# A weight's float built in place in SBUF, its low part formed by GpSimd, the skip score's product in a bank of its own, and a new table for the planner

## The chip, the cores and the metric

The kernel runs on one core of one Trainium2 chip. The core has five engines that run side by side, each through its own queue in order: TensorE (PE in the profile) multiplies matrices, VectorE (DVE), ScalarE (ACT) and GpSimd (POOL) work element by element, and SyncE (SP) issues the transfers between HBM and SBUF. Products land in PSUM, which has eight banks of 512 floats for each of 128 partitions. The metric is the device time of one execution in microseconds; less is better.

## The reference

Three layers follow each other. Shapes: batch 4, 8 heads, 768 positions, head size 48, so 3072 tokens of width 384; the middle layer is 2048 wide.

```python
# 1: a recurrence with a complex decay for each head and channel
mag = np.sqrt(a_re * a_re + a_im * a_im)
scale = np.minimum(mag, 0.999) / (mag + 1e-06)
...
    S_re, S_im = (new_re + kv, new_im)
    y[:, :, t] = np.einsum('bhd,bhde->bhe', q[:, :, t], S_re)
# 2: a wide layer with a rational function
h = x @ w_in
P = a[0] + a[1] * h + a[2] * h2 + a[3] * h3
Q = 1.0 + np.abs(b[0]) * np.abs(h) + np.abs(b[1]) * h2
g = P / (Q + 1e-06)
return (g @ w_out).astype(np.float32)
# 3: experts, for those tokens alone whose skip score is above 0
skip_score = x @ w_skip
do_compute = skip_score > 0
```

## The kernel before

The tokens are cut into 24 chunks of 128; two chunks are a unit, so there are 12 units. For each unit the first layer runs in chunk form. An "early" chain (e1 to e13, ScalarE and VectorE in turn, lines 442 to 453) forms logarithms and angles of the decay; an arc tangent (L484) and two sines (L478, L479) follow, each with a reload of ScalarE's function table; TensorE forms prefix sums (L545 to L575); key and query products kt and qt (L327), transposes (L619) with their evictions (L625), scores (L637), masks, products with v and the state (L663, L665) and the update of the state (L684) give y. GpSimd, VectorE or ScalarE then split y into a high and a low part (xh, xl; L716 to L721).

The second layer runs in steps: 8 for a unit, 96 in all, each for 256 tokens and 256 of the 2048 middle channels. G1 (L766) is two groups of nine products (three inputs times high-high, low-high, high-low), G2 (L812) two groups of six that are accumulated in two PSUM banks `ob` over a unit's 8 steps. Between them stand, for each step, ScalarE's a1 to a5 (L752, L324), VectorE's d1 to d4 (L756) and the split into gh (L795) and gl (L798). The step buffers are threefold: G1 of step s+3 waits for d4 of step s. The first step's G1 needs xh and xl of both chunks of unit 0. The other six PSUM banks, `zb`, are handed out by the planner.

The weights are float64 in memory. The function `weight` turns each piece of 128 x 384 into a float32 and splits it into a high and a low part (wih, wil, woh, wol). A double's two 32-bit words lie side by side: `lw` and `hw` are views with a stride of two words over the staging buffer. wb1 (L353) and wb2 (L356) gather low bits and sign in a `zb` bank, wy (L360) scales the upper word, wb3 (L363) joins both into that bank, whi (L371) rounds it to the high part, wlo (L373) subtracts. There are 16 pieces of w_in (steps 0 to 7, two each) and 16 of w_out, so 32 in all, and all of them belong to the first unit.

The order on every engine is decided when the kernel is built: `Plan.order` plays the tasks through with a cost for each choice of engine, a due time and the numbers of the table `PP` (slacks, biases, engines ruled out for a task in `NO`, due times of steps), and the instructions are emitted in the order it finds. So a changed cost or table changes the order on all engines.

At a unit's end, ScalarE or VectorE evicts the two `ob` banks to `x2b` (named ev), which is stored; sk (L330) multiplies `ob` by w_skip in place and sums it into `skip`. After the last unit `flags` adds up what the later paths would have to do; in the trace no instruction of them runs.

Of the kernel before, what the change touches and what calls it, by code (L numbers as in the profile page):

```python
# [10 lines left out]
F32 = mybir.dt.float32  # L11
# [146 lines left out]
PP = dict(P0=5.749, P1=7.419, NO={'kr': ('ACT', 'POOL'), 'wy': ('ACT', 'DVE'), 'e4': ('ACT',), 'ev': ('POOL',), 'xabs': ('DVE',), 'cadd8': ('DVE',), 'xpe': ('POOL',), 'xlo': ('ACT',), 'msk': ('POOL',), 'whi': ('POOL',), 'qr': ('ACT', 'DVE'), 'prr2': ('DVE',), 'prr1': ('ACT', 'DVE'), 'gh': ('ACT', 'DVE'), 'cadd': ('ACT', 'DVE'), 'gl': ('DVE',), 'yev': ('DVE',)}, E0=-7.632, E1=-9.777, TC=40, WS=(0, 1, 2, 3, 4, 5, 0, 1, 1, 0, 1, 2, 2, 1, 2, 2), HO={('d2b', 'ACT'): 0.618, ('msk', 'ACT'): 0, 'DVE': 0.349, 'POOL': 0}, DW=88.344, WL=9, P=5.802, LAG2=4.955, SL={'ACT': 0.3, 'DVE': 3.115, 'POOL': 1.396, 'SP': 1.011, 'PE': 1.871, '2': 2.358}, X1=13.588, T0=107.458, NZ=6, NH=3, CU=2, BI={'DVE': 7.051, 'POOL': 17.078})  # L158


def main_part(tc, ctx, q, k, v, a_re, a_im, w_in, w_out, moe_a, moe_b, w_skip, out, keep):
# [176 lines left out]
    def weight(keys, tag, stg, hi, lo, key, part, shape=lambda x: x):  # L338

        n = DM  # L340
        h_, w_ = (tag + ("h",), ("wz", tag[0], part % 2))
        tk = ("wz",) + key
        if wide:
            rw = stg.bitcast(I32).rearrange("p (n z) -> p n z", z=2)
            lw, hw = rw[:, :, 0], rw[:, :, 1]
            hf = hw.bitcast(F32)

            def bits():
                return zb[pl.slot[tk]][:, 0:n].bitcast(I32)
# [13 lines left out]
            pl.add([("DVE", 0.48, lambda: nc.vector.scalar_tensor_tensor(  # L363
                out=bits(), in0=hw, scalar=3, in1=bits(), op0=ALU.logical_shift_left, op1=ALU.bitwise_or))],
                reads=keys + [h_], writes=[w_], name="wb3")
            src, fr = [w_], tk
        else:
            def t():
                return shape(stg)
            src, fr = keys, None  # L370
# [58 lines left out]
    def early(u, cc):  # L429
        load_a(u, cc)  # L430
        w = len(cc) / 2
        fa, fd, fp = 0.73 if w == 1 else 0.43, 0.87 if w == 1 else 0.47, 1.76 if w == 1 else 0.94
# [56 lines left out]
    def cums(u, c):  # L489
# [7 lines left out]
        if not first and not summed:  # L497
            cr = cs[0:1, hs, 1, :]
            pl.add(dma((cr, xr[127:128, ps, :])), reads=[f"x{1 - c}"], writes=[f"cs{c}"], name=f"cry{ci}", xfer=0.03)
            def a0():  # L500
                return hd("ai", F32, u)[0:1, hs, :]

            def cadd():
                nc.gpsimd.tensor_scalar(out=cr, in0=cr, scalar1=-2.0 * math.pi, scalar2=1.0, op0=ALU.mult, op1=ALU.mult)
                nc.gpsimd.tensor_tensor(out=a0(), in0=a0(), in1=cr, op=ALU.add)
            pl.add([("POOL", 1.3, cadd), ("DVE", 0.5, lambda: nc.vector.scalar_tensor_tensor(
                out=a0(), in0=cr, scalar=-2.0 * math.pi, in1=a0(), op0=ALU.mult, op1=ALU.add), True)],
                   reads=[f"cs{c}"], writes=[f"ai{c}"], name="cadd")
# [5 lines left out]
        if split and c == 0:  # L514
# [12 lines left out]
            pl.add([("POOL", 0.92, lambda: thi("POOL")), ("ACT", 0.73, lambda: thi("ACT")),  # L527
# [63 lines left out]
        if ci % CPB != CPB - 1:  # L591
            pl.add([("POOL", 0.5, lambda: nc.gpsimd.tensor_copy(last[96:128], r1[96:128, c].rearrange("p h d -> p d h")))],
                   reads=[f"r1{c}"], writes=["last"], name="last")
            pl.add(dma(*[(dec[ci % ND][48 * z:48 * z + 48, :], last[127:128]) for z in range(2)]), reads=["last"], writes=[("dec", ci % ND)], name=f"dec{ci}")

    def qrkr(u):
        for c in range(2):
            hs = slice(8 * c, 8 * c + 8)
            pl.add([tt("POOL", 0.96, r1[:, c], r1[:, c], raw["q"][:, hs, :], ALU.mult),
                    tt("DVE", 0.47, r1[:, c], r1[:, c], raw["q"][:, hs, :], ALU.mult)],  # L600
                   reads=["q"], writes=[f"r1{c}"], name="qr")

    def prods(u, c):
        ci = 2 * u + c
        csl = cs[:, 8 * c:8 * c + 8]
        for nm, r, t, key in (("r2", r2, kt[ci % 2], ("kt", ci % 2)), ("r1", r1, qt[0], "qt")):
            i0 = r[:, c].unsqueeze(2).to_broadcast([128, 8, 2, 48])
            pl.add([tt("DVE", 0.87, t, i0, csl, ALU.mult), tt("POOL", 1.76, t, i0, csl, ALU.mult)],
                   reads=[f"{nm}{c}", f"cs{c}"], writes=[key], name="pr" + nm)
# [21 lines left out]
    def scores(ci, hf):  # L631
# [14 lines left out]
        pl.add([("POOL", 0.6, lambda: nc.gpsimd.affine_select(  # L646
# [49 lines left out]
    def yevac(ci):  # L696
# [45 lines left out]
    def step(s):  # L742
# [76 lines left out]
        if p == NP - 1:  # L819
            for t in range(2):  # L820
# [8 lines left out]
                pl.add([stt(0.55, o, o, fine["sg"], wsk, ALU.mult, ALU.mult, both=False, accum_out=skip[:, ti:ti + 1])],  # L829
                       reads=["wsk", "cf"], writes=[("o", t)], name="sk", due=at(1, 3))  # L830
# [435 lines left out]
```

## Time and profile before

| | us |
|---|---|
| median of 3 runs (669.85 to 672.43) | 672.06 |
| the profiled execution: its own time | 673.5 |
| its span, first to last instruction | 671.8 |
| TensorE busy | 615.5 (92%) |
| ScalarE busy | 570.0 (85%) |
| VectorE busy | 498.8 (74%) |
| GpSimd busy | 470.7 (70%) |

A row's duration contains overlap with its neighbours on the same engine, so a group of rows can be shorter than its sum. A bracket at a row's end gives the idle time of the engine before it and what ended that. "PEclk" or the granted clock is the share of TensorE's full clock; the mean over the span is 0.962.

### The profile page before, as it was taken

The page shows a single profiled execution, that of the slowest core. Times are in us where ns is not written, and L with a number is a line of the kernel's source. Part 1 is how long each engine was busy: PE and PEld are TensorE (multiplying, and loading weights), DVE is VectorE, ACT ScalarE, POOL GpSimd, SP SyncE. Part 2 cuts the span into 40 slices and gives each one's busy share as a digit, 9 for nine tenths or more (in the row PEclk, how much of TensorE's full clock was granted, in tenths as well). Part 3 has the DMA queues.
Part 4 walks back from the last instruction along what each step waited for, and adds up shares of the span by engine and source line. Part 5 has one row for each costly group of instructions (what it writes and reads, how often), then busy time and mean ns, then how long its engine had stood idle before and what let it go on. Part 6 is the DMA issues. An engine that isn't in the chain of part 4 may idle for free.

```text
span 671.8 us, 13043 instructions
## 1 busy us (share of the span) xinstructions
PE 615.5 (92%) x4772; PEld 586.5 (87%) x4772; DVE 498.8 (74%) x822; ACT 570.0 (85%) x962; POOL 470.7 (70%) x469
## 2 busy tenths in 40 slices
PE   0485599999999999999999999999999999999993
PEld 0273489999999999999999999999989999999993
DVE  6989979977768877776689687686598676565771
ACT  5858988997999998997999998997999996976770
POOL 5566567787887696875887797775977776754452
PEclk9758879999999999999999999999999999999998
DMA  9834232410311212111212112111213010000000
GB/s 304 294 108 135 72 105 64 145 36 18 97 36 47 67 39 76 48 27 53 70 39 84 28 40 68 44 40 52 60 40 98 13 40 4 1 27 4 13 13 30
DMA packets 52140, 43.32 MB, mean 64 GB/s; under 512 B 31201, under 2 KB 48993, under 8 KB 52065
## 3 DMA queue, kind: packets, MB, share of 16 engines
q1 hardware_dynamic: 52064, 42.38, 20.9%
q8 instruction: 39, 0.64, 0.4%
q14 instruction: 37, 0.30, 0.1%
HBM read 36.38 MB, written 4.72 MB: 61 GB/s over the span
## 4 chain that ended last, share of the span: by engine, by line
PE 79%; DVE 8%; ACT 7%; issue 2%; DMA 2%; POOL 1%; SPq 0%; POOLq 0%; ACTq 0%
PE zb L766 28%; PE ob L812 28%; PE zb L637 6%; PE zb L619 5%; PE zb L663 4%; PE zb L684 3%; PE zb L665 2%; DVE wk L756 1%; DMA xl<-in_moe_w_out_dram 1%; ACT wk L752 1%; DVE zb L353 1%; DVE ail L537 1%; PE zb L575 1%; DVE zb L363 1%; DVE ta L445 1%
## 5 line engine op out<-in xcount | busy, mean ns | idle before, releaser
L756 DVE SCALAR_TENSOR_TENSOR wk<-wk,cf,zb 128x512 f32<-128x512 f32 x192 | 142.4, 743 | 105.2 <-ACT zb L752 49.1
L766 PE MATMUL zb<-xh,wih 128*128 128x256 f32 x576 | 167.6, 291 | 8.2 <-DVE wk L756 8.2
L766 PE MATMUL zb<-xl,wih 128*128 128x256 f32 x576 | 163.4, 284 | 0.0
L766 PE MATMUL zb<-xh,wil 128*128 128x256 f32 x576 | 162.7, 282 | 0.0
L324 ACT ACTIVATE wk<-wk,cf 128x512 f32<-128x512 f32 x192 | 139.0, 724 | 1.5
L798 POOL TENSOR_TENSOR gl<-wk,gh 128x512 fp32r<-128x512 f32 x96 | 131.8, 1374 | 5.8
L812 PE MATMUL ob<-woh,gh 128*128 128x384 f32 x384 | 134.5, 350 | 0.0
L812 PE MATMUL ob<-woh,gl 128*128 128x384 f32 x384 | 130.3, 339 | 0.0
L812 PE MATMUL ob<-wol,gh 128*128 128x384 f32 x384 | 130.3, 339 | 0.0
L795 POOL TENSOR_SCALAR gh<-wk 128x512 fp32r<-128x512 f32 x96 | 64.0, 667 | 83.3 <-PE ob L812 67.0
L766 PEld LDWEIGHTS zb<-xh,wih 128*128 128x128 f32 x576 | 109.5, 190 | 11.8 <-DVE wk L756 8.4
L766 PEld LDWEIGHTS zb<-xl,wih 128*128 128x128 f32 x576 | 109.5, 190 | 0.3 <-POOL wk L360 0.3
L766 PEld LDWEIGHTS zb<-xh,wil 128*128 128x128 f32 x576 | 109.7, 190 | 0.0
L752 ACT ACTIVATE wk<-zb 128x512 f32<-128x512 f32 x96 | 57.2, 595 | 29.4 <-PE zb L766 28.5
L812 PEld LDWEIGHTS ob<-woh,gh 128*128 128x128 f32 x384 | 72.9, 190 | 2.4 <-issue 2.4
L812 PEld LDWEIGHTS ob<-wol,gh 128*128 128x128 f32 x384 | 73.1, 190 | 0.0
L812 PEld LDWEIGHTS ob<-woh,gl 128*128 128x128 f32 x384 | 72.7, 189 | 0.0
L756 DVE SCALAR_TENSOR_TENSOR zb<-wk,cf,zb 128x512 f32<-128x512 f32 x96 | 71.8, 748 | 0.0
L756 DVE SCALAR_TENSOR_TENSOR wk<-wk,zb 128x512 f32<-128x512 f32 x96 | 65.4, 682 | 1.7
L752 ACT ACTIVATE wk<-zb,cf 128x512 f32<-128x512 f32 x96 | 65.4, 681 | 0.8 <-POOL gl L798 0.6
L752 ACT ACTIVATE zb<-wk 128x512 f32<-128x512 f32 x96 | 57.8, 602 | 7.2 <-DVE wk L756 6.8
L637 PE MATMUL zb<-qT,kT 96*128 96x128 f32 x384 | 51.6, 284 | 1.5 <-ACT qT L625 1.5
(164 smaller groups left out, 1251.0 us busy)
## 6 DMA issues: line engine op xcount, KB each, us to landing
wk<-in_moe_w_in_dram SPq DMA_DIRECT2D x8, 768.0 KB
ar<-in_a_re_dram SPq DMA_DIRECT2D x24, 192.0 KB, 2.5
ai<-in_a_im_dram SPq DMA_DIRECT2D x24, 192.0 KB, 3.1
kraw<-in_k_dram SPq DMA_DIRECT2D x24, 192.0 KB, 2.5
qraw<-in_q_dram SPq DMA_DIRECT2D x24, 192.0 KB, 4.1
vb<-in_v_dram SPq DMA_DIRECT2D x24, 192.0 KB, 3.1
out_dram<-x2b SPq DMA_DIRECT2D x24, 192.0 KB, 1.9
xl<-in_moe_w_out_dram SPq DMA_DIRECT2D x5, 384.0 KB
```

Of the source, the lines that this page charges most:

```text
L324: return ("ACT", cost, lambda: nc.scalar.activation(out=out, in_=in_, func=func, **kw))
L619: nc.tensor.transpose(z[0:96, i, :], src[:, 4 * hf + i].rearrange("p z d -> p (z d)"), ident)
L637: nc.tensor.matmul(z[:, i, :], lhsT=kT[hf][:, i, :], rhs=qT[hf][:, i, :], start=True, stop=True)
L663: nc.tensor.matmul(dst, lhsT=vt[:, h, :], rhs=pT[hf][:, i, :], start=True, stop=first)
L665: nc.tensor.matmul(dst, lhsT=state[:, h, :], rhs=qT[hf][:, i, :], start=False, stop=True)
L684: nc.tensor.matmul(z[:, h, :], lhsT=ktc[:, h].rearrange("p z d -> p (z d)"), rhs=vt[:, h, 0:48], start=True, stop=True)
L752: return ("ACT", cost, lambda: nc.scalar.activation(out=h() if out is None else out, in_=h() if in_ is None else in_, func=func, **kw))
L756: return ("DVE", cost, lambda: nc.vector.scalar_tensor_tensor(out=h() if out is None else out, in0=in0, scalar=scalar, in1=h(), op0=op0, o ...
L766: nc.tensor.matmul(h()[:, i * 256:i * 256 + 256], lhsT=w[:, j, fs], rhs=x[:, j, :], start=(n == 0), stop=(n == 8))
L795: nc.gpsimd.tensor_scalar(out=g, in0=uu, scalar1=1.0, scalar2=1.0, op0=ALU.mult, op1=ALU.mult)
L798: eng[e].tensor_tensor(out=ghl("gl", s), in0=uu, in1=ghl("gh", s).bitcast(F32), op=ALU.subtract)
L812: nc.tensor.matmul(o, lhsT=a[:, sl], rhs=w[:, f, :], start=(f == 0 and n == 0), stop=(f == NF - 1 and n == 2))
```

## The change

wb3 now writes the finished float over the upper word in the staging buffer instead of into the `zb` bank, which is free after it. whi and wlo read it there. wlo may run on GpSimd or VectorE; the new table leaves GpSimd. wy may run on ScalarE or GpSimd. sk writes its product into a `zb` bank. Several costs of the planner are different, "last" may run on ScalarE too, and the table `PP` is another one.

```diff
-PP = dict(P0=5.749, P1=7.419, NO={'kr': ('ACT', 'POOL'), 'wy': ('ACT', 'DVE'), 'e4': ('ACT',), 'ev': ('POOL',), 'xabs': ('DVE',), ...
+PP = dict(P0=2.588, P1=7.659, NO={'kr': ('ACT', 'POOL'), 'wy': ('DVE',), 'e4': ('ACT', 'POOL'), 'xabs': ('DVE', 'POOL'), ...
...
             def t():
-                return shape(zb[pl.slot[tk]][:, 0:n])
+                return shape(hf)
...
             pl.add([act(0.42, hf, hf, AF.Copy, scale=2.0 ** -112),
-                    ("POOL", 0.45, lambda: nc.gpsimd.tensor_scalar(
+                    ("POOL", 0.57, lambda: nc.gpsimd.tensor_scalar(
                         out=hf, in0=hf, scalar1=2.0 ** -112, scalar2=1.0, op0=ALU.mult, op1=ALU.mult))],
                    reads=keys + [w_], writes=[h_], name="wy")
-            pl.add([("DVE", 0.48, lambda: nc.vector.scalar_tensor_tensor(
-                out=bits(), in0=hw, scalar=3, in1=bits(), op0=ALU.logical_shift_left, op1=ALU.bitwise_or))],
-                reads=keys + [h_], writes=[w_], name="wb3")
-            src, fr = [w_], tk
+            pl.add([("DVE", 0.47, lambda: nc.vector.scalar_tensor_tensor(
+                out=hw, in0=hw, scalar=3, in1=bits(), op0=ALU.logical_shift_left, op1=ALU.bitwise_or))],
+                reads=keys + [w_], writes=[h_], free=tk, name="wb3")
+            src = keys + [h_]
...
-        pl.add([("DVE", 0.48, lambda: nc.vector.tensor_tensor(out=lo, in0=t(), in1=hi.bitcast(F32), op=ALU.subtract))],
-               reads=[("wh",) + key] + ([] if wide else keys), writes=[("wl",) + key] + ([w_] if wide else []), free=fr,
-               name="wlo")
+
+        def wlo(e):
+            eng[e].tensor_tensor(out=lo, in0=t(), in1=hi.bitcast(F32), op=ALU.subtract)
+        pl.add([("POOL", 1.02, lambda: wlo("POOL")), ("DVE", 0.47, lambda: wlo("DVE"), True)],
+               reads=[("wh",) + key] + src, writes=[("wl",) + key], name="wlo")
...
-                pl.add([stt(0.55, o, o, fine["sg"], wsk, ALU.mult, ALU.mult, both=False, accum_out=skip[:, ti:ti + 1])],
-                       reads=["wsk", "cf"], writes=[("o", t)], name="sk", due=at(1, 3))
+                sk_ = ("zk", ti)
+                pl.add([("DVE", 0.65, lambda o=o, ti=ti, sk_=sk_: nc.vector.scalar_tensor_tensor(
+                    out=zb[pl.slot[sk_]][:, 0:DM], in0=o, scalar=fine["sg"], in1=wsk, op0=ALU.mult, op1=ALU.mult,
+                    accum_out=skip[:, ti:ti + 1]))],
+                       reads=["wsk", "cf", ("o", t)], bank=sk_, free=sk_, name="sk", due=at(1, 3))
```

The order moves on every engine. Three places follow; a line number of the kernel after is 2 to 7 higher than that of before.

SyncE, the first transfers of the program, before (ar and ai are the decay's two parts, wk the staging buffer that holds w_in):

```order
L320 DMA wk<-in_moe_w_in_dram 128x1536
L320 DMA ar_158<-in_a_re_dram 128x384
L320 DMA ai_159<-in_a_im_dram 128x384
L320 DMA ar_158<-in_a_re_dram 128x384
L320 DMA ai_159<-in_a_im_dram 128x384
L320 DMA wk<-in_moe_w_in_dram 128x1536
L320 DMA kraw<-in_k_dram 128x384 x2
```

and now:

```order
L320 DMA ar_157<-in_a_re_dram 128x384
L320 DMA ai_158<-in_a_im_dram 128x384
L320 DMA ar_157<-in_a_re_dram 128x384
L320 DMA ai_158<-in_a_im_dram 128x384
L320 DMA kraw<-in_k_dram 128x384 x2
L320 DMA qraw<-in_q_dram 128x384 x2
L320 DMA wk<-in_moe_w_in_dram 128x1536 x2
```

The decay of unit 0 now goes first, keys and queries next, the first two pieces of w_in behind them. VectorE's and ScalarE's queues follow: their first rows are the early chain of unit 0, without a weight in between.

GpSimd, behind the constants, now (r is a decay factor that becomes a product with k or q, qraw the queries; the subtractions of L375 stood on VectorE before, as L373):

```order
L360 TENSOR_SCALAR wk<-wk 128x384 x2
L375 TENSOR_TENSOR wil<-wk,wih 128x3x128
L360 TENSOR_SCALAR wk<-wk 128x384
L375 TENSOR_TENSOR wil<-wk,wih 128x3x128
L595 COPY last<-r_106 32x384
L375 TENSOR_TENSOR wil<-wk,wih 128x3x128
L327 TENSOR_TENSOR r_106<-r_106,qraw 128x384
L360 TENSOR_SCALAR xl_1_130<-xl_1_130 128x384
L360 TENSOR_SCALAR xh_0_129<-xh_0_129 128x384
L271 TENSOR_SCALAR na<-ar_bc 128x4
L327 TENSOR_TENSOR kt_111<-r_108,cs 128x768
L327 TENSOR_TENSOR qt_110<-r_106,cs 128x768
```

Three subtractions and the scalings of five pieces stand ahead of kt and qt of chunk 0; the key product of chunk 1 (kt_112), which stood further down this queue before, is on VectorE now.

TensorE, the instructions that end in the first G2 product (L812, now L816), before:

```order
L766 MATMUL zb_86<-xh_8_492,wih 128x256
L766 MATMUL zb_86<-xl_9_497,wih 128x256
L766 MATMUL zb_86<-xh_8_492,wil 128x256
L812 MATMUL ob_81<-woh,gh_677 128x384
L812 MATMUL ob_81<-wol,gh_677 128x384
```

and now:

```order
L688 MATMUL zb_88<-vb_101,kt_111 96x48 x8
L547 MATMUL zb_84<-ta_749,trir 128x384
L548 MATMUL zb_84<-ail,trir 128x384
L623 MATMUL zb_88<-ident,qt_110 96x128 x4
L623 MATMUL zb_84<-ident,qt_110 96x128 x4
L641 MATMUL zb_88<-qT_113,kT_115 128x128 x4
L574 MATMUL zb_88<-tb_703,trir 128x384
L575 MATMUL zb_88<-ar_722,trir 128x384
L641 MATMUL zb_84<-qT_114,kT_116 128x128 x4
L816 MATMUL ob_81<-woh,gh_802 128x384
```

Before, eight G1 groups (steps 0 to 3) lead straight to the first G2. Now six G1 groups (steps 0 to 2) are followed by the transposes, scores, state products and state update of chunk 2, and by the transposes and scores of chunk 3, and then comes the first G2.

## Rows read from the trace of the kernel before

**Rows 1.** Stretches of the span: busy us of each engine, clock, transfers.

```profile
core 0: us, PE busy (x) PEld busy (x) DVE busy (x) ACT busy (x) POOL busy (x), PEclk, DMA share, GB/s
0.00:100.00 100.00, 55.96 (x303) 44.91 (x304) 86.93 (x178) 74.50 (x128) 57.60 (x83) 0.78 0.53 171
27.00:73.20 46.20, 33.45 (x201) 26.70 (x202) 42.52 (x85) 32.61 (x58) 28.37 (x32) 0.70 0.45 145
120.00:660.00 540.00, 538.32 (x4276) 522.21 (x4275) 391.01 (x605) 476.64 (x801) 397.24 (x368) 1.00 0.16 46
```

**Rows 2.** Waits of TensorE: total us, times, longest.

```profile
PE zb L548 <- ACT ai L484: 15.9, 1, 15.9
...
PE zb L766 <- DVE wk L756: 8.2, 1, 8.2
...
PE zb L546 <- DVE ail L537: 1.0, 2, 0.5
```

**Rows 3.** Timeline of TensorE: start, us, instruction.

```profile
86.49 0.52 PE L812 MATMUL ob<-woh,gh 128*128 128x384 f32 x1
...
120.20 0.34 PE L812 MATMUL ob<-woh,gh 128*128 128x384 f32 x1
```

**Rows 4.** Timeline of ScalarE.

```profile
14.97 0.84 ACT L484 ACTIVATE ai<-ai 128x768 f32<-128x768 f32 x1
...
26.01 0.92 ACT L479 ACTIVATE cs<-cs,halfpi 128x768 f32<-128x768 f32 x1
...
72.61 0.60 ACT L752 ACTIVATE zb<-wk 128x512 f32<-128x512 f32 x1
```

**Rows 5.** The chain that ended last: start, us, piece.

```profile
56.80 0.93 DVE zb L353 x2
...
82.48 4.21 PE zb L766 x18
86.69 3.08 PE ob L812 x12
...
100.65 0.89 PE zb L637 x8
...
107.54 1.32 PE zb L684 x16
...
123.85 1.08 PE zb L766 x9
...
143.39 2.09 PE ob L812 x12
...
580.73 1.31 PE zb L619 x12
...
661.12 0.59 ACT x2b L324
...
661.74 0.69 DVE ob L330 x2
```

**Rows 6.** Groups of instructions: names, shape, count; busy us, mean ns; idle before.

```profile
L373 DVE TENSOR_TENSOR wil<-zb,wih 128x384 fp32r<-128x384 f32 x16 | 8.5, 551 | 2.6 <-ACT wih L371 2.6
...
L721 POOL TENSOR_TENSOR xl<-ys,xh 128x384 fp32r<-128x384 f32 x20 | 20.5, 1025 | 9.8 <-ACT xh L716 3.8 <-ACT x2b L324 3.4 <-DVE xh L718 2.2
...
L537 DVE SCALAR_TENSOR_TENSOR ail<-ai,ta 128x384 fp32r<-128x384 f32 x20 | 19.7, 983 | 7.2 <-ACT ta L532 5.4 <-POOL ta L534 1.4
```

**Rows 7.** Timeline of VectorE.

```profile
6.48 0.55 DVE L451 TENSOR_SCALAR_CACHE_REDUCE ar<-ar 128x384 f32<-128x384 f32 x1
...
27.11 1.72 DVE L297 TENSOR_TENSOR cf<-cf 128x2 f32<-128x2 f32 x1
...
349.49 2.62 DVE L537 SCALAR_TENSOR_TENSOR ail<-ai,ta 128x384 fp32r<-128x384 f32 x1
...
556.28 0.55 DVE L537 SCALAR_TENSOR_TENSOR ail<-ai,ta 128x384 fp32r<-128x384 f32 x1
```

**Rows 8.** Transfers by line: count, KB each, median us from issue to landing.

```profile
ar<-in_a_re_dram SPq DMA_DIRECT2D x24, 192.0 KB, 2.5
```

**Rows 9.** Timeline of GpSimd.

```profile
27.01 1.80 POOL L327 TENSOR_TENSOR kt<-r,cs 128x768 f32<-128x768 f32 x1 [1.72 <-ACT cs L479]
```

More of the change, by code (lines that the diff above doesn't have):

```diff
@@ L431, in early @@
         w = len(cc) / 2
-        fa, fd, fp = 0.73 if w == 1 else 0.43, 0.87 if w == 1 else 0.47, 1.76 if w == 1 else 0.94
+        fa, fd, fp = 0.73 if w == 1 else 0.43, 0.87 if w == 1 else 0.47, 1.8 if w == 1 else 0.95
         hs = slice(8 * cc[0], 8 * cc[-1] + 8)
@@ L505, in cadd @@
                 nc.gpsimd.tensor_tensor(out=a0(), in0=a0(), in1=cr, op=ALU.add)
-            pl.add([("POOL", 1.3, cadd), ("DVE", 0.5, lambda: nc.vector.scalar_tensor_tensor(
+            pl.add([("POOL", 1.55, cadd), ("DVE", 0.5, lambda: nc.vector.scalar_tensor_tensor(
                 out=a0(), in0=cr, scalar=-2.0 * math.pi, in1=a0(), op0=ALU.mult, op1=ALU.add), True)],
@@ L526, in tlo @@
                                      op=ALU.subtract)
-            pl.add([("POOL", 0.92, lambda: thi("POOL")), ("ACT", 0.73, lambda: thi("ACT")),
+            pl.add([("POOL", 0.82, lambda: thi("POOL")), ("ACT", 0.73, lambda: thi("ACT")),
                     ("DVE", 0.45, lambda: thi("DVE"), True)], reads=["ta0", "ta1"], writes=["tb0", "tb1"], name="thi")
@@ L591, in cums @@
         if ci % CPB != CPB - 1:
-            pl.add([("POOL", 0.5, lambda: nc.gpsimd.tensor_copy(last[96:128], r1[96:128, c].rearrange("p h d -> p d h")))],
+            r_last = r1[96:128, c].rearrange("p h d -> p d h")
+            pl.add([("POOL", 0.88, lambda: nc.gpsimd.tensor_copy(last[96:128], r_last)),
+                    ("ACT", 0.65, lambda: nc.scalar.activation(out=last[96:128], in_=r_last, func=AF.Copy))],
                    reads=[f"r1{c}"], writes=["last"], name="last")
@@ L598, in qrkr @@
             hs = slice(8 * c, 8 * c + 8)
-            pl.add([tt("POOL", 0.96, r1[:, c], r1[:, c], raw["q"][:, hs, :], ALU.mult),
+            pl.add([tt("POOL", 1.04, r1[:, c], r1[:, c], raw["q"][:, hs, :], ALU.mult),
                     tt("DVE", 0.47, r1[:, c], r1[:, c], raw["q"][:, hs, :], ALU.mult)],
@@ L607, in prods @@
             i0 = r[:, c].unsqueeze(2).to_broadcast([128, 8, 2, 48])
-            pl.add([tt("DVE", 0.87, t, i0, csl, ALU.mult), tt("POOL", 1.76, t, i0, csl, ALU.mult)],
+            pl.add([tt("DVE", 0.87, t, i0, csl, ALU.mult), tt("POOL", 1.83, t, i0, csl, ALU.mult)],
                    reads=[f"{nm}{c}", f"cs{c}"], writes=[key], name="pr" + nm)
@@ L645, in scores @@
             reads=[tk], writes=[f"p{hf}"], free=tk, name="msk")
-        pl.add([("POOL", 0.6, lambda: nc.gpsimd.affine_select(
+        pl.add([("POOL", 0.7, lambda: nc.gpsimd.affine_select(
             out=pT[hf], in_=pT[hf], pattern=[[0, 4], [1, 128]], base=0, channel_multiplier=-1,
@@ L723, in due @@
             return start(NP * u) - PP["X1"] - (PP["E0"], PP["E1"], 0.0)[min(u, 2)]
-        pl.add([("DVE", 0.47, lambda: xhi("DVE")), ("ACT", 0.45, lambda: xhi("ACT"))],
+        pl.add([("DVE", 0.4, lambda: xhi("DVE"), True), ("ACT", 0.45, lambda: xhi("ACT"))],
                reads=["ys"], writes=[("xh", u % 2, c)], name="xhi", due=due)
-        pl.add([("POOL", 0.96, lambda: xlo("POOL")), ("DVE", 0.47, lambda: xlo("DVE"))],
+        pl.add([("POOL", 0.99, lambda: xlo("POOL")), ("DVE", 0.47, lambda: xlo("DVE"), True)],
                reads=["ys", ("xh", u % 2, c)], writes=[("xl", u % 2, c)], name="xlo", due=due)
@@ L798, in glo @@
             eng[e].tensor_tensor(out=ghl("gl", s), in0=uu, in1=ghl("gh", s).bitcast(F32), op=ALU.subtract)
-        pl.add([("POOL", 0.59, lambda: ghi("POOL")), ("DVE", 0.34, lambda: ghi("DVE"), True), ("ACT", 0.52, lambda: ghi("ACT"))],
+        pl.add([("POOL", 0.63, lambda: ghi("POOL")), ("DVE", 0.34, lambda: ghi("DVE"), True), ("ACT", 0.52, lambda: ghi("ACT"))],
                reads=[U], writes=[GH], name="gh", late=True)
-        pl.add([("POOL", 1.23, lambda: glo("POOL")), ("DVE", 0.6, lambda: glo("DVE"), True)], reads=[U, GH], writes=[GL],
+        pl.add([("POOL", 1.3, lambda: glo("POOL")), ("DVE", 0.6, lambda: glo("DVE"), True)], reads=[U, GH], writes=[GL],
                name="gl", late=True)
```

8 lines of the change are left out of this document (4 added, 4 removed).

## The prediction, before the change was run

> **What bounds the kernel now.** I read the stretches first. From 120 to 660 us TensorE is busy 538.3 of 540 us at a granted clock of 1.00 [rows 1], so there the time is the sum of its products and little else. In the first 100 us it is busy 56.0 us, at a mean clock of 0.78, while VectorE is busy 86.9 us. So the change can win what TensorE loses before about 120 us, and what stands behind its last product.
>
> The waits of TensorE say where it loses [rows 2]: 15.9 us for the arc tangent of the first unit, 8.2 us at the end of the first three steps, for the VectorE operation that frees a buffer of step 0; in the rest of the kernel the largest kind is 1.0 us in two waits. The timeline gives the marks [rows 3]: the first G2 product (L812) starts at 86.49, the first G2 product of step 3 at 120.20. On ScalarE [rows 4] the arc tangent ends at 15.81, the second sine of unit 0 at 26.93 and the second Exp of step 0 (L752, zb<-wk) at 73.21.
>
> From here on I count in TensorE's work. The chain view prices it at full clock [rows 5]: a G1 group (nine products) 1.08 us, a G2 group (six) 2.09/12 x 6 = 1.05, four transposes 0.44 (1.31 for three such sets), a head group of scores 0.89, a state update 1.32. By these prices and the order of before, the work between 86.49 and 120.20 is 28.9 us and took 33.7, so 4.8 were lost to half clock and waits there. After that hardly anything is lost.
>
> **What the change does to the engines, term by term.**
>
> *Weights.* 32 pieces. Each loses one VectorE subtraction (L373, 0.55 us a row) and gets one on GpSimd. VectorE's rows overlap: two of them take 0.93 us of the chain [rows 5], so 0.465 each and 32 x 0.465 = 14.9 us off VectorE. On GpSimd the nearest row is the subtraction of the same shape in L721, 1.03 us [rows 6]: 32.8 us on. The scaling (L360) goes from GpSimd to ScalarE for 16 of the 32 and is counted in ScalarE's queue below. L363 now writes SBUF instead of PSUM; it still has one PSUM operand, and I keep 0.465. Had the strided write a price of its own it would be bounded by the 0.55 of the whole row, 32 x 0.09 = 2.7 us, half of it in the stretch that counts.
>
> *The table.* It moves more than the weights do. By instruction counts, 21 of 24 key products (kt), 39 of 96 gl, 11 e4 and 8 carry additions go from GpSimd to VectorE; 11 transposes' evictions, 11 evictions of the output and 8 xh go from VectorE to ScalarE. From 120 us on VectorE is busy 391 of 540 us and ScalarE 477 [rows 1]. VectorE gets some 44 us net by unlocked prices and stands near 81%, ScalarE near 89%. Both stay under TensorE's 540, so I cost this at nothing; the cover is the three steps by which G1 runs ahead of G2. If it fails, that is the rival below.
>
> *The start.* Before, a weight is transferred first, and the first a_re is used at 6.48, behind that weight's first operations [rows 7]. Now a_re and a_im are issued first; with the median 2.5 us to landing [rows 8] from an issue at 0.8 the first is there near 3.4, and VectorE has nothing but the early chain in its queue until it is through. The chain from the first use to the end of the arc tangent took 9.3 us with weights in between (6.48 to 15.81); without them, and with e4 on VectorE, I count 7.3: arc tangent done near 10.7. From there to the sines took 11.1; ScalarE now has a scaling and an Exp more in between, 12 us: 22.6 against 26.93. The coefficients still block on GpSimd's kt and qt: L297 took 1.72 us beside the 1.80 of kt [rows 7, 9].
>
> *From the sines to the first G2.* This stretch decides. In the new order VectorE has, from L297 to the d2 of step 0: 58 weight operations (27.0), 12 wide operations of the early chain (13.5), three kt (2.7), coefficients (4.7), six xr and r2 (2.8), five of the state (2.4), four step operations (2.7), five others (3.2): 59 us. ScalarE has 94 instructions, 57 us (each of both sums at the start-to-start time that its kind has in the trace). Before, in the 46.2 us from 27 to 73.2, VectorE was busy 42.5, 92% [rows 1], ScalarE 71%. At VectorE's 92%, 59 us take 64 and end at 86.7; because two queues near their limit now wait for each other I add 2 and take 89. Then d2, d3 and d4 follow in a row (2.05), gh and gl on GpSimd (0.67 + 1.37): **first G2 near 93**, later than the 86.49 of before.
>
> But more lies behind it. Ahead of their first G2 both orders put the same attention work of unit 0; after it, before has 8 G1 groups (8.7), the new order 6 (6.5) and nearly all TensorE work of chunk 2 and the first half of chunk 3: 8 transpose sets 3.5, four score groups 3.6, the state products 2.0, an update 1.3, three pairs of prefix sums 1.1, changes of format 0.2, together 11.7. So it has 9.5 us more done: gain 86.5 + 9.5 - 93.1 = **2.9**.
>
> *After the first G2.* Before lost 4.8 there. The waits for transposes and scores of chunk 2 go away with their being earlier. What can stay is a restart at half clock: at 82.48 two G1 groups took 4.21 instead of 2.16 [rows 5], and the G2 behind them 3.08 instead of 2.09: 3.0. Taken whole: gain **1.8** (0 to 4.8).
>
> *The skip score.* Its product goes to a free bank, so that it need not wait until ScalarE has read ob. Behind the last product, the second one started 0.62 after ScalarE's eviction did (661.12, 661.74) [rows 5]; now it can start with it: **0.5**. In the middle it hides under TensorE's 538 of 540.
>
> Sum: 2.9 + 1.8 + 0.5 = 5.2. The profiled execution: 671.8 - 5.2 = 666.6 of span, 668.3 with the 1.7 around it. The median of the runs shown (672.06) lies 1.4 below the profiled 673.5, so I predict **667**.
>
> **Bounds.** If the two queues pack without a hole, 22.6 + 59 = 81.6, first G2 at 85.7, with no loss behind it: gain 10.3 + 4.8 + 0.5 = 15.6, 656. If ScalarE's 57 us run at the 71% of before, they take 80, first G2 at 107: 11 lost, 1.8 and 0.5 won, 681. The 92% is nearer because ScalarE's idle time there was waiting for a full VectorE queue, which has lost 15 us of weight work.
>
> **Rivals.**
> 1. *The queues hardly wait, TensorE keeps its clock through the attention work ahead of the first G2.* For it: the order has little left that waits on GpSimd, whose queue in that stretch is shorter. Against it: 71% of before. 656 to 663, say 660. Chance 0.17.
> 2. *The gain is eaten.* At 85% the 59 us take 69.4; with the same 2 and 4.1 the first G2 starts at 98 and 2 are lost against before; with the 1.8 and 0.5 the total stands where it did: 672. For it: the early lead is paid by later work put ahead of step 0. Chance 0.25.
> 3. *Slower: VectorE and GpSimd block each other from 120 us on.* The 1x384 ail (L537) takes 0.55 us free, 0.98 on the mean and 2.62 at 349.49, beside GpSimd's gl [rows 6, 7]; that one held TensorE for half a microsecond, and its place against the work done slipped by 1.0. The change gives VectorE some 84 more operations with both inputs in SBUF; at the mean 0.43 of waiting each that is 36 us, VectorE near 87%, and a cluster at a unit's end can be late. Ten units at 1.0 us: 667 + 10 = 677. It decides once more than 8.5 us of new TensorE waits stand behind 120 us. Against it: GpSimd gives away 39 gl, 21 kt and 11 e4 there and is less often in the way. Chance 0.20.
>
> [...]
>
> **Numbers.** Forecast (663 to 668.7) 0.38, rival 1 0.17, rival 2 0.25, rival 3 0.20. Half a per cent (3.4 us) is about what a measurement of this kernel can tell from no change: faster 0.38 + 0.17 = 0.55, the same 0.25, slower 0.20. Range 658 to 677: it leaves out the end of rival 1 and the upper half of rival 3.
>
> **What the profile would show.** Arc tangent's end near 10.7 and sines' near 22.6: the start. First G2 near 93 with chunk 2's scores ahead of it: the middle. TensorE busy over 99% from 120 us on: the cover. New waits of TensorE for kt, ail or d4 behind 120 us: rival 3. A first G2 at 98 or later, with ScalarE or VectorE idle over 15% between the sines and it, is rival 2 and would make the forecast wrong, as would L363 or the GpSimd subtraction at well over 0.55 and 1.1 us.

## The result, and the profile of the kernel after

The median went from 670.95 us (668.76 to 672.43) to **678.01 us** (675.75 to 681.10): a ratio of 1.0101, with a 95% interval of 1.0072 to 1.0130. The change makes the kernel 1.0% slower. 667 was forecast, with a range of 658 to 677.

The profiled execution after took 675.75 us (span 673.8), the quickest of its four; that of before, 673.5, lies above its four. So the two profiles differ by 2.0 us of span where the medians differ by 7. A second trace of each order's start, which comes with the experiments, closes most of that gap.

The stretches, with the columns of [rows 1]; the fifth line reaches from the end of the sines to the start of step 0's d3, which follows d2:

```profile
0.00:100.00 100.00, 57.92 (x333) 45.16 (x334) 86.03 (x161) 84.92 (x147) 66.68 (x87) 0.77 0.55 174
27.00:73.20 46.20, 31.62 (x188) 26.31 (x187) 43.20 (x83) 37.83 (x67) 32.22 (x34) 0.67 0.48 150
100.00:120.00 20.00, 20.00 (x162) 19.39 (x162) 18.02 (x32) 17.49 (x33) 12.05 (x14) 0.96 0.31 100
120.00:160.00 40.00, 38.97 (x326) 37.17 (x326) 33.69 (x53) 37.33 (x64) 28.28 (x27) 1.00 0.19 49
24.48:94.15 69.67, 47.15 (x306) 38.88 (x306) 62.93 (x111) 60.81 (x107) 50.93 (x49) 0.74 0.44 138
160.00:660.00 500.00, 497.69 (x3938) 483.51 (x3937) 407.81 (x602) 443.52 (x745) 268.42 (x271) 1.00 0.15 43
```

VectorE, which lost 32 subtractions, is as busy in the first 100 us as before (86.0 beside 86.9 [rows 1]); ScalarE has gained 10.4 us there, GpSimd 9.1. From 160 us on TensorE is busy 99.5% of the time, about as before [rows 1].

TensorE's waits, answering to [rows 2]:

```profile
PE zb L550 <- ACT ai L486: 12.3, 1, 12.3
PE zb L623 <- POOL kt L327: 5.5, 1, 5.5
PE zb L641 <- ACT qT L629: 4.5, 4, 2.5
PE zb L770 <- ACT xh L720: 4.4, 1, 4.4
PE zb L623 <- ACT kT L629: 3.8, 2, 2.0
PE zb L623 <- DVE kt L327: 2.2, 4, 0.7
```

The wait for the arc tangent is 3.6 us shorter and the 8.2 for VectorE's d4 is gone. In their place stand 12.7 us of waits for ScalarE: two kinds of evicted transposes and xh. Two more waits of before's start belong to the comparison; [rows 2], and with them the prediction, leave them out:

```profile
PE zb L575 <- DVE ta L445: 8.7, 3, 5.0
PE zb L619 <- POOL kt L327: 7.1, 1, 7.1
```

They are 1.7 (two waits, ta) and 5.5 us now. All waits of TensorE together come to 47.4 us before and 46.8 after, so it does not wait longer than before.

The marks, from the timelines of TensorE, ScalarE and VectorE [rows 3, 4, 7]: the scores ahead of the first G2 and that G2, the end of the arc tangent and of the sines, a5 of step 0 (its second Exp) and d2, the last skip score with the eviction behind which it stands, and a key product beside GpSimd:

```profile
98.66 1.91 PE L641 MATMUL zb<-qT,kT 96*128 96x128 f32 x8
100.22 0.67 PE L816 MATMUL ob<-woh,gh 128*128 128x384 f32 x1
...
3.37 0.55 DVE L453 TENSOR_SCALAR_CACHE_REDUCE ar<-ar 128x384 f32<-128x384 f32 x1 [3.37 <-DMA ar<-in_a_re_dram]
5.54 0.55 DVE L453 TENSOR_SCALAR_CACHE_REDUCE ar<-ar 128x384 f32<-128x384 f32 x1 [1.61 <-DMA ar<-in_a_re_dram]
11.40 0.84 ACT L486 ACTIVATE ai<-ai 128x768 f32<-128x768 f32 x1
23.56 0.92 ACT L481 ACTIVATE cs<-cs,halfpi 128x768 f32<-128x768 f32 x1
76.06 2.11 DVE L327 TENSOR_TENSOR kt<-r,cs 128x768 f32<-128x768 f32 x1
92.84 0.61 ACT L756 ACTIVATE zb<-wk 128x512 f32<-128x512 f32 x1
93.49 0.75 DVE L760 SCALAR_TENSOR_TENSOR wk<-wk,cf,zb 128x512 f32<-128x512 f32 x1
...
663.18 0.58 ACT L324 ACTIVATE x2b<-ob,cf 128x384 f32<-128x384 f32 x1 [0.46 <-PE ob L816]
663.80 0.62 DVE L834 SCALAR_TENSOR_TENSOR zb<-ob,cf,wsk 128x384 f32<-128x384 f32 x1 [0.36 <-ACT x2b L324]
```

The groups that the change touches [rows 6], one line of before first, since it is not shown above:

```profile
L371 ACT ACTIVATE wih<-zb 128x384 fp32r<-128x384 f32 x16 | 7.2, 486 | 0.0
```

and after:

```profile
L371 ACT ACTIVATE wih<-wk 128x384 fp32r<-128x384 f32 x16 | 8.4, 543 | 2.2 <-DVE wk L363 2.2
L363 DVE SCALAR_TENSOR_TENSOR wk<-wk,zb 128x384 int32<-128x384 int32 x17 | 9.1, 548 | 0.3 <-POOL wk L360 0.2
L375 POOL TENSOR_TENSOR wil<-wk,wih 128x384 fp32r<-128x384 f32 x16 | 17.3, 1091 | 5.4 <-ACT wih L371 3.0 <-DVE xl L363 2.3
L327 DVE TENSOR_TENSOR kt<-r,cs 128x768 f32<-128x768 f32 x21 | 29.6, 1441 | 3.0 <-ACT cs L481 3.0
```

**Lost time.** To compare orders I use one measure: at a mark, the clock minus TensorE's work ahead of the mark at full clock. The work is counted with the prices of the prediction, and for the kinds that it did not price with estimates from rows of before: 0.85 for a product of the fp32 prefix sums (two of its rows take 0.88 at 56.58 and 0.91 at 20.90), 0.135 for one with v and 0.115 for one with the state (near half of the 0.26 and 0.23 that four rows take from start to start at 403.64 and 403.90), and some 0.04 for each change of format (the four rows with v take 0.27 behind one at 405.93 and 0.22 without one at 406.42), of which before has 180 and after 186. Both orders then hold the same total, 592.6 and 592.9 us. At its first G2 the kernel before has 29.1 us of work behind it, so 86.5 - 29.1 = 57.4 are lost; the one after has 38.5, so 61.7.

| lost us at | first G2 | G2 of step 3 | of step 7 | of step 95 |
|---|---|---|---|---|
| before | 57.4 | 62.2 | 62.2 | 68.3 |
| before's start, second trace | 57.4 | 60.1 | 60.1 | |
| after | 61.7 | 62.5 | 64.4 | 70.1 |
| after, second trace | 63.6 | 64.7 | 66.6 | 72.3 |

From step 7 to the end before loses 6.1 us and after 5.7: the long dense part is no different. The whole difference arises ahead of step 7. With the second traces, which lie nearer to the medians, it is 66.6 - 60.1 = 6.5 us.

Lost time is either idle time or products that take longer than their price at full clock. Up to the first G2, before and after:

```profile
0.00:86.49 86.49, 43.91 (x234) 33.53 (x235) 77.33 (x162) 63.56 (x109) 47.87 (x74) 0.78 0.57 186
0.00:100.22 100.22, 58.14 (x334) 45.38 (x335) 86.25 (x161) 84.92 (x147) 66.90 (x87) 0.77 0.55 173
```

TensorE is idle for 42.6 us before and 42.1 after (42.4 and 43.3 in the second traces). What grew is the other part: 43.9 - 29.1 = 14.8 us above price before, 58.1 - 38.5 = 19.6 after. The 9.4 us of work that the new order puts ahead of the first G2 kept TensorE busy for 14.2. This is an account and not yet a cause: with faster products, part of that time might have been waiting for the other engines instead.

### The profile page after: what moved, and what is told of

It reads as the page before. It is cut to its first block, busy times and chain, and to the rows that moved or that the text cites. A ratio compares the mean times of both kernels' runs of the same rounds, so it can differ in the third digit from the quotient of the medians.

```text
span 673.8 us, 13019 instructions
## 1 busy us (share of the span) xinstructions
PE 617.9 (92%) x4772; PEld 588.2 (87%) x4772; DVE 547.8 (81%) x852; ACT 584.4 (87%) x989; POOL 375.4 (56%) x396
## 4 chain that ended last, share of the span: by engine, by line
PE 77%; DVE 8%; ACT 7%; issue 2%; POOL 2%; DMA 1%; SPq 1%; POOLq 0%; ACTq 0%
PE zb L770 28%; PE ob L816 27%; PE zb L641 6%; PE zb L623 5%; PE zb L667 4%; PE zb L688 3%; PE zb L669 2%; DVE gl L802 1%; ACT tb L444 1%; DVE kt L327 1%; DMA wk<-in_moe_w_in_dram 1%; POOL gh L799 1%; DVE zb L356 1%; DVE zb L353 1%; PE zb L574 1%
## 5 line engine op out<-in xcount | busy, mean ns | idle before, releaser
L816 PE MATMUL ob<-woh,gh 128*128 128x384 f32 x384 | 133.1, 347 | 0.0
L816 PE MATMUL ob<-woh,gl 128*128 128x384 f32 x384 | 129.8, 338 | 0.0
L816 PE MATMUL ob<-wol,gh 128*128 128x384 f32 x384 | 129.7, 338 | 0.0
L802 POOL TENSOR_TENSOR gl<-wk,gh 128x512 fp32r<-128x512 f32 x57 | 80.2, 1408 | 4.3
L816 PEld LDWEIGHTS ob<-woh,gh 128*128 128x128 f32 x384 | 72.5, 189 | 1.2 <-issue 1.0
L816 PEld LDWEIGHTS ob<-wol,gh 128*128 128x128 f32 x384 | 72.5, 189 | 0.0
L816 PEld LDWEIGHTS ob<-woh,gl 128*128 128x128 f32 x384 | 72.3, 188 | 0.0
L641 PE MATMUL zb<-qT,kT 96*128 96x128 f32 x384 | 55.5, 295 | 8.0 <-ACT qT L629 4.5
```

Source lines behind the costliest of these rows:

```text
L641: nc.tensor.matmul(z[:, i, :], lhsT=kT[hf][:, i, :], rhs=qT[hf][:, i, :], start=True, stop=True)
L802: eng[e].tensor_tensor(out=ghl("gl", s), in0=uu, in1=ghl("gh", s).bitcast(F32), op=ALU.subtract)
L816: nc.tensor.matmul(o, lhsT=a[:, sl], rhs=w[:, f, :], start=(f == 0 and n == 0), stop=(f == NF - 1 and n == 2))
```

## The experiments

Each was timed in five or more rounds beside the kernel before. "In its order" means that the planner still sees the old task, so every instruction keeps its place and only its engine or operand is another.

**The changed kernel once more.**

> The changed kernel once more, to see where its time goes in another execution. Its profiled execution (673.8 us of span) was the quickest of four (676.4, 679.2 and 675.9 for the others), with the highest granted clock (0.960 beside 0.953 to 0.955). Theory A (the loss sits ahead of the dense part: ScalarE and VectorE are both full there and TensorE runs at half clock when it is fed late): 676 to 680 us, the first G2 product at 100 to 106 us, and TensorE's waits behind 120 us still under 4 us. Rival B (VectorE and GpSimd block each other in the dense part): the same time, but the first G2 product stays at 100 and new TensorE waits of 5 us or more stand behind 120 us.

678.05 us, ratio 1.0103 [1.0077, 1.0130]. First G2 at 102.11; TensorE's waits behind 120 us come to 3.0 us. Theory A holds, and B falls (the 3.0 leave out the last 1.7, of `flags`). Of the 2.2 us between this trace and the first one 1.9 arise ahead of the first G2, as the table above shows.

**The table alone.**

```
 # weight() and the skip score as before; PP and the other costs as after
```

> The new table and the new costs, but the weight's float in PSUM, its low part on VectorE and the skip score in place, as before. Theory A (the order that the new table makes is what costs, the code edits are worth under 1.5 us either way): 675 to 685 us; it stays slower than before, by the 14.9 us of subtractions that VectorE keeps perhaps more so. Rival C (the subtractions on GpSimd and the in-place float are what costs): 668 to 672, no slower than before.

688.22 us, ratio 1.0253 [1.0222, 1.0285]. Slower as A says, beyond its range. TensorE's waits between 60 and 115 us mostly name VectorE's subtractions:

```profile
PE zb L768 <- DVE wol L373: 7.2, 2, 4.1
PE zb L621 <- DVE wol L373: 5.1, 1, 5.1
```

**The weight edit alone, low part on GpSimd, old table.**

```
 # PP and costs as before, but
+NO = {..., 'wlo': ('DVE',)}
 # weight() as after; skip score as before
```

> The old table and the old costs, with the weight's float built in SBUF and its low part on GpSimd alone; the skip score in place as before. Theory A: 666 to 673 us, no slower than before by more than 2, although GpSimd gets 32 more operations of 1.0 us in the first 100 us. Rival C: 676 us or more, with VectorE or GpSimd operations of the start visibly stretched and the first G2 product 5 us or more behind the 86.5 of before at the same work done.

681.12 us, ratio 1.0147 [1.0118, 1.0176]. Theory A fails: the edit is not harmless under the old table. Rival C has the time but not the place. At step 3 only 60.8 us are lost, which lies between the two traces of before; 4.9 more go between steps 3 and 7, where TensorE waits 2.9 us for a key product on GpSimd (L621 <- POOL kt), and 10.5 behind step 7.

**Low part back on VectorE, in the new order.**

```
-pl.add([("POOL", 1.02, lambda: wlo("POOL")), ...
+pl.add([("POOL", 1.02, lambda: wlo("DVE")), ...
```

> The changed kernel with its order kept place for place, but the 32 low parts of the weights on VectorE where they stood on GpSimd. Theory A (VectorE and ScalarE are full ahead of the first G2): VectorE gets 14.9 us more, so the first G2 product goes from 100 to 105 or later and the time to 680 to 690. Rival C (the GpSimd subtraction is what costs): the first G2 product at 95 or earlier and 670 to 674 us.

683.47 us, ratio 1.0182 [1.0153, 1.0211]; first G2 at 106.87. Theory A holds: in this order the subtractions on GpSimd are worth some 5 us, and that edit does what the prediction took it to do. VectorE is then without a gap:

```profile
60.00:80.00 20.00, 13.27 (x69) 11.40 (x68) 20.00 (x37) 16.22 (x27) 7.31 (x7) 0.74 0.56 183
```

**Scalings from ScalarE to GpSimd, in the new order; more work for ScalarE; more work for VectorE.**

```
-pl.add([act(0.42, hf, hf, AF.Copy, scale=2.0 ** -112),
+pl.add([("ACT", 0.42, lambda: nc.gpsimd.tensor_scalar(out=hf, in0=hf, scalar1=2.0 ** -112, scalar2=1.0, ...
```

```
-lambda: nc.scalar.activation(out=hi, in_=t(), func=AF.Copy)
+lambda: [nc.scalar.activation(out=hi, in_=t(), func=AF.Copy) for _ in range(2 if key[0] == "i" else 1)]
```

The third repeats wb2 on VectorE in the same way.

> The changed kernel with its order kept place for place, but the weights' scalings that it put on ScalarE (16 or so, 0.45 us each) on GpSimd instead. Theory D (ScalarE, busy 92% from 40 to 100 us, has become the engine that sets when the Exp and d4 of step 0 come): some 7 us less in ScalarE's queue move the first G2 product from 100 to 102 (the two looks of it) to 95 to 97, and the time from 678 to 672 to 675. Rival E (VectorE, busy 88% with operations stretched by GpSimd, sets it): no gain, 677 to 681, since GpSimd gets 16 more operations of 0.55 and VectorE's wb3 then waits for GpSimd's queue.

> The changed kernel in its own order, with the rounding to the high part on ScalarE made twice for the 16 pieces of w_in, to the same result: 16 x 0.45 = 7.2 us more in ScalarE's queue, all ahead of the first G2. Theory D (ScalarE sets the pace there): first G2 5 to 7 us later, 683 to 686 us. Rival E (VectorE sets it): first G2 at most 2 us later, 678 to 680 us.

> The changed kernel in its own order, with the sign operation (wb2) on VectorE made twice for the 16 pieces of w_in, to the same result: 16 x 0.465 = 7.4 us more in VectorE's queue, all ahead of the first G2. Theory D: first G2 at most 2 us later, 678 to 681 us. Rival E: first G2 6 to 9 us later, 684 to 687 us. If both kernels with doubled work are slower by most of what was added, both queues set the pace in turn.

Ratios 1.0135 [1.0105, 1.0165], 1.0175 [1.0143, 1.0207] and 1.0161 [1.0128, 1.0193]; first G2 at 103.57, 106.87 and 107.86, beside 100.22 and 102.11. Theory D fails in the first and third, E in the second. Adding 7.2 us to ScalarE or 7.4 to VectorE puts the first G2 back by 4.8 and 5.8 from the later of the two marks, and the median by 5.6 and 5.1: most of what was added, so both queues set the pace in turn. Taking the scalings off ScalarE helps nothing, but GpSimd is full then, so that run does not tell what a shorter ScalarE queue alone would be worth. The same stretch in the changed kernel itself, and then in the three:

```profile
60.00:80.00 20.00, 11.43 (x73) 9.82 (x71) 19.88 (x33) 18.51 (x31) 17.42 (x16) 0.83 0.56 175
...
60.00:80.00 20.00, 11.22 (x66) 9.49 (x66) 17.68 (x32) 14.51 (x22) 19.80 (x20) 0.83 0.58 187
...
60.00:80.00 20.00, 12.33 (x82) 10.35 (x79) 18.96 (x35) 18.99 (x34) 16.24 (x17) 0.83 0.53 174
...
60.00:80.00 20.00, 12.25 (x80) 10.37 (x77) 19.79 (x37) 17.05 (x31) 13.49 (x15) 0.83 0.54 168
```

VectorE (third column) is full already without added work, 19.88 of 20. Given the work, GpSimd (fifth) rises from 17.42 to 19.80 and ScalarE (fourth) from 18.51 to 18.99, level with VectorE. None of the three has much room to give.

**The skip score's bank alone, old table.**

```
-pl.add([stt(0.55, o, o, fine["sg"], wsk, ...
+pl.add([("DVE", 0.65, ... out=zb[pl.slot[sk_]][:, 0:DM], in0=o, ...))], ..., bank=sk_, free=sk_
```

> The kernel before with the skip score's product in a bank of its own and nothing else; the order on TensorE stays the same as before up to the end of the first unit's steps. The prediction gave this edit 0.5 us at the end: 670 to 671 us. Rival: the bank that it takes at a unit's end comes from the six that the planner hands out, and the steps there wait for it: 672 us or more. Its start is also a second look at the start of the kernel before: first G2 near 86.5.

676.97 us, ratio 1.0080 [1.0051, 1.0109]: the rival's side. But the waits that name the product in the bank come to 0.6 us (0.3 each of G1 and of transposes); between step 7 and the end 10.6 us are lost, beside 6.1 before. Its start is the second trace of the table: the same order, first G2 at 86.45, but 2.1 us less lost by step 3. From the first G2 on the two traces of before's start differ in the granted clock, this one first:

```profile
80.00:100.00 20.00, 16.03 (x108) 15.33 (x109) 17.57 (x31) 18.37 (x31) 16.22 (x15) 0.84 0.36 109
```

```profile
80.00:100.00 20.00, 16.05 (x87) 15.39 (x88) 16.09 (x28) 16.70 (x28) 13.01 (x13) 0.70 0.36 109
```

The first product of that G2 takes 0.33 us here and 0.52 in the other trace [rows 3]. What an added bank costs is thus not separated from the order that it makes.

**One cost changed by 0.01, under either table.**

```
-pl.add([("DVE", 0.46, lambda: nc.vector.tensor_scalar(out=bits(), in0=lw, ...   # wb1, before
+pl.add([("DVE", 0.47, ...
```

> The kernel before with one of the planner's costs raised by 0.01 (that of wb1, from 0.46 to 0.47, as the change also does): the same code, the same table, the same operations, but another order from the 141st row of TensorE on. Theory F (the old table fits the old costs and code, and any edit that makes the planner reorder loses what that fit was worth): 674 to 681 us, as far from 671 as the edits of the weight (681) and of the skip score (677) under the old table. Rival G (those two edits cost by what they do, not by the order that they make): 670 to 672.5.

> The changed kernel with the same cost lowered by 0.01 (0.47 to 0.46); another order from the 219th row of TensorE on. Theory F with the new table fitted to the new code in the same way: 681 to 687 us. If the new table fits nothing in particular: 675 to 681, as likely below as above the 678 of the changed kernel.

675.62 us, ratio 1.0044 [1.0022, 1.0066], and 676.77, ratio 1.0077 [1.0052, 1.0103]. Reordering alone costs the kernel before 0.4%, some 3 us, with no operation changed: theory F's direction and range hold, by less than the edits under the old table cost (10 and 5 us). For the new table it fails: a neighbouring order is no slower.

**The skip score in place again, in the new order.** It writes its product over the bank that it reads; where the order puts it ahead of an eviction, the stored rows hold that product.

```
-out=zb[pl.slot[sk_]][:, 0:DM], in0=o,
+out=o, in0=o,
```

> The changed kernel in its own order, with the skip score's product written back over its own bank as before (the planner still sets a bank aside). Theory F: the edit itself is worth nothing, 677 to 679, and behind the last product the second skip score starts 0.62 us after ScalarE's eviction, as in both kernels so far. Rival (the separate bank frees the accumulator bank earlier at each unit's end): 680 us or more, with new waits of the first G2 product of a unit. Rival G (the bank of its own is what costs 5 us): 673 to 675.

678.71 us, ratio 1.0097 [1.0068, 1.0127]. In this order the bank is worth nothing either way.

**All of the code, old table.**

> The whole code edit (weight in place, low part on GpSimd or VectorE as the planner likes, skip score in a bank) under the old table: the fourth of the four cases of old and new code and table. Theory F: 676 to 684, slower than before although it takes 8 us or more off VectorE. Rival H (the table is the loss and the code a gain): 664 to 670.

686.65 us, ratio 1.0219 [1.0187, 1.0252]; F by its direction, above its range, and H falls. TensorE waits for GpSimd between 100 and 165 us:

```profile
PE zb L621 <- POOL kt L327: 4.9, 1, 4.9
PE ob L814 <- POOL gl L800: 1.5, 1, 1.5
```

So the four cases are 1, 1.025 (table alone), 1.022 (code alone) and 1.010 (both). Code and table belong together. By the waits shown, the old table leaves the key products on GpSimd, which is late once it has subtractions too (23 of the 32 there); the new one gives them to VectorE, which is late unless the subtractions leave it.

**Extra products in TensorE's waits, in either order.**

```
+for _ in range(WARM.get(n, 0)):   # n: TensorE's n-th task
+    nc.tensor.matmul(ob[0][:, 0:128], lhsT=tri, rhs=tri, start=True, stop=True)
```

> The changed kernel in its own order, with 47 extra products of constants (128x128, into an accumulator bank that is not used yet) put on TensorE's queue into the waits that its trace shows ahead of the first G2 product: they fill TensorE's waits and change nothing that is computed. Theory K (much of what the start loses is TensorE at half clock: the granted clock is 0.50 from 23 to 40 us and 0.74 to 0.83 from 40 to 100, and its products feed both full queues): the clock in those stretches at 0.9 or more, the first G2 product at 95 to 98, 671 to 674 us. Theory D+E (VectorE and ScalarE set the pace whatever TensorE's clock is): first G2 within 1.5 us of the 100 to 102 of before, 677 to 680 us.

> The kernel before in its own order, with 57 extra products of constants in TensorE's waits in the same way. Theory K: its median falls by 2 to 4 us to 667 to 669, and its runs spread less, since the two looks at its start (clock 0.60 and 0.81 from 20 to 60 us in the one, 1.00 in the other) differ by 2.1 us of lost time at the first G2 of step 3. Theory D+E: 670 to 672, no change.

676.24 us, ratio 1.0067 [1.0043, 1.0091], and 672.30, ratio 1.0005 [0.9984, 1.0026]. In the changed kernel the extra products did not raise the clock from 40 to 80 us (0.77 and 0.83, beside 0.74 and 0.83 in its first trace and 0.77 and 0.83 in its second), and the first G2 stands at 100.84. Theory K's forecast fails, but the condition it rests on was not met, so the run does not tell what a higher clock would be worth there.

In the kernel before they did raise it: 0.86 from 23 to 40 us, 1.00 and 0.97 from 40 to 80, beside 0.53, 0.81 and 0.79 in the first trace. The update of the state at 39 us took 1.48 us instead of 2.79, ScalarE waited 0.30 instead of 2.38 for the scores behind it, and the first G2 stands at 82.90 instead of 86.49. First before, then with the extra products:

```profile
39.42 2.79 PE L684 MATMUL zb<-vb,kt 128*96 128x48 f32 x16
44.09 0.60 ACT L644 ACTIVATE pT<-zb 128x512 f32<-128x512 f32 x1 [2.38 <-PE zb L637]
```

```profile
39.11 1.48 PE L685 MATMUL zb<-vb,kt 128*96 128x48 f32 x16
41.59 0.60 ACT L645 ACTIVATE pT<-zb 128x512 f32<-128x512 f32 x1 [0.30 <-PE zb L638]
```

So theory K's mechanism is seen in that execution (669.56 us), against theory D+E's "whatever TensorE's clock is"; yet the median gains nothing. No version here is faster than the kernel before.

## Why the prediction was wrong, step by step

The sum, in us of gain, against the traces:

| step | forecast | first trace | second traces |
|---|---|---|---|
| arc tangent done, sines done | 10.7, 22.6 | 12.24, 24.48 | 12.24, 24.48 |
| VectorE's work to d2 of step 0 | 59 | 62.9 busy in 69.7 | 63.2 busy in 71.6 |
| a5 of step 0 done | 89 | 93.45 | 95.37 |
| first G2 | 93 | 100.22 | 102.11 |
| gain at the first G2 | 2.9 | -4.3 | -6.2 |
| gain behind it, to step 7 | 1.8 | 2.1 | -0.3 |
| dense part | 0 | 0.4 | |
| skip score | 0.5 | 0.0 | |
| sum | 5.2 | -1.8 | -6.5 to step 7 |

**The step that failed is the stretch from the sines to the first G2**, the one that the prediction said decides. Its mechanism is nearest to rival 2: the gain is eaten, first G2 at 98 or later, though VectorE and ScalarE were idle 10 and 13% of the stretch and not over the 15 that rival 2 named. The work moved ahead of the first G2 was sized rightly (9.4 us for 9.5) and the mark was not. Three terms of it were short.

*The start, 1.9 us.* The first a_re landed at 3.37, as forecast; the second half was first used at 5.54, after 1.61 us of waiting for its transfer, which the estimate left out. The sines came 2.4 us earlier than before, not 4.3.

*The sum of 59, some 4 us.* VectorE was busy 62.9 us. Wide operations with both inputs in SBUF were stretched while GpSimd ran: the key product at 76.06 took 2.11, beside GpSimd's qt from 74.80 to 77.36, against 0.95 for the one at 34.03, while the wb2 at 75.59, with one input in PSUM, took 0.55 beside the same qt; the surplus over the free durations is some 4.3 us in ten rows of the stretch. The prediction priced such stretching for the dense part (rival 3) and for the coefficients, not for this stretch. Over the whole kernel the 21 key products on VectorE took 1.44 on the mean. VectorE's idle time was as forecast, 6.7 us beside 7.4 (22.6 + 59 = 81.6, and 89 was taken).

*From a5 to the first G2, 2.6 us.* Forecast 4.1 behind the end of a5, for d2 to gl. gl ended at 97.86, but TensorE then had a prefix sum and a head group of scores (eight rows) ahead of G2 in its order, until 100.22; the scores took 1.91 us where the prediction's price is 0.89. From the start of a5 to the first G2 it is 7.4 us in both traces (92.84 to 100.22, 94.76 to 102.11) and in the runs with the low part on VectorE, the scalings on GpSimd and more work for ScalarE (99.43 to 106.87, 96.20 to 103.57, 99.46 to 106.87), and 6.9 with more work for VectorE (101.01 to 107.86): that it hardly moves speaks for the order, which no run changed there. TensorE's work ahead of G2 was counted as a gain at full clock; that it runs at a granted clock of 0.74 in this stretch, and part of it late, was not.

**Which engine.** The prediction followed VectorE's queue and took ScalarE's as the slower bound. ScalarE is busy 60.8 of the 69.7 us, and the runs with added work show that each of the two sets the pace. Summed over 0 to 120 us, where both kernels stand at the first G2 of step 3 (120.20 and 121.02), the three elementwise engines are busy 271.6 us before and 285.2 after (VectorE 105.9 and 104.1, ScalarE 92.2 and 102.4, GpSimd 73.5 and 78.7). The 14.9 us taken off VectorE came back as key products, e4 and stretched rows, and ScalarE got the evictions and scalings. One cost was missed outright: rounding the high part reads SBUF instead of PSUM and takes 543 instead of 486 ns, 32 x 0.057 = 1.8 us on ScalarE.

**What held.** wb3's strided write costs nothing (548 ns beside the 553 of the same group before); the GpSimd subtraction is 1.09 beside the 1.03 assumed; from 120 us on VectorE is some 50 us busier (33.7 + 407.8 = 441.5 beside 391.0 [rows 1]) with no more loss behind step 7, so rival 3 falls.

**Luck.** Behind the first G2 the gain was 2.1 for 1.8 in the first trace, but it is not the one described: less is lost to step 3 (0.8 instead of 4.8), and 1.9 go to step 7 that were not lost before, with waits for key products on VectorE and one eviction. In the second traces before loses 2.7 there and after 3.0, so the agreement does not repeat.

**The skip score.** The eviction of the same bank still comes first: 663.18 to 663.80 is the 0.62 of before [rows 5], because the instruction waits in the program for ScalarE's eviction whatever it writes. The diff changes the output, not that wait.

**The level.** The forecast was made against a profile above the median and took off 1.4 us for it. That was right for before; but after's own executions spread from 675.75 to 681.10, and between two traces of one order 2.1 to 2.2 us differ ahead of step 3. For before that goes with the granted clock from the first G2 on (0.84 and 0.70 above). For after it goes with TensorE's clock too: the second trace falls behind where the same products run at half pace (granted clock 0.79 and 0.57 from 83 to 91 us), and ScalarE, which evicts them, then waits. First trace, then second:

```profile
83.03 1.16 PE L641 MATMUL zb<-qT,kT 96*128 96x128 f32 x8 [1.71 <-ACT pT L648]
88.05 0.60 ACT L629 ACTIVATE kT<-zb 96x512 f32<-96x512 f32 x1
```

```profile
83.75 2.08 PE L641 MATMUL zb<-qT,kT 96*128 96x128 f32 x8 [1.70 <-ACT pT L648]
89.64 0.59 ACT L629 ACTIVATE kT<-zb 96x512 f32<-96x512 f32 x1 [0.61 <-PE zb L623]
```

So of the 1.9 us by which the first G2 of one and the same order moved, 0.7 stood already at these products (83.03 and 83.75), and 1.2 came behind them, with a granted clock of 0.57 instead of 0.79 up to 91 us.

What stays open: how much of the loss against before is that clock and how much the three full engines, since no run raised the changed kernel's clock; and how the 10 and 5 us of the weight edit and the bank under the old table divide between the new order (3 us for a mere reorder) and the work itself, since no run kept the old order with these edits.

## What to carry to other kernels

When a change takes work off the busiest of several engines that feed one another, add up the busy time of all of them over the stretch, before and after; if the sum grows, the gain must come from packing, and that is what has to be shown. Price the stretching of one engine's rows beside another's (here 2.11 us for 0.95) wherever both are full, not only where it was seen. Work that is moved into a stretch of low clock is to be priced at that clock: here 9.4 us of products kept TensorE busy for 14.2, at a granted clock of 0.77 up to there. Where a planner orders everything, change one operation in its kept place to learn what it is worth: a cost moved by 0.01 shifted this kernel by 0.4%.

## What the runs showed of the hardware that was not expected

The two traces of before's start differ in the granted clock from 20 to 40 us, 1.00 and 0.60, the second trace first:

```profile
20.00:40.00 20.00, 9.65 (x32) 6.07 (x31) 19.20 (x51) 13.45 (x24) 10.81 (x14) 1.00 0.50 182
39.63 2.79 PE L684 MATMUL zb<-vb,kt 128*96 128x48 f32 x16
```

```profile
20.00:40.00 20.00, 9.11 (x33) 6.06 (x32) 19.20 (x51) 13.77 (x25) 11.05 (x14) 0.60 0.51 184
```

Their products run alike there: the update of the state takes 2.79 us in both, and 1.48 with the extra products, where the column has 0.86 from 23 to 40 us. So in these traces the column alone does not tell how fast the products ran.

Filling TensorE's waits raised its clock in one kernel and not in the other: from 40 to 60 us 1.00 beside 0.81 in the kernel before, 0.77 beside 0.74 and 0.77 in the changed one. In the changed kernel the extra products ahead of the first real one end at 7.2 us, TensorE then waits 5.33 us, and the first four rows of real products take 2.90 us with them and without.
